# Top-k attention with a GELU block: turn copies, projections and the first pair's load put in another order

## The chip, the cores and the metric

The kernel runs on one core of a Trainium2 chip. The time is the device time of one execution in microseconds (us); the median of several executions is given. A core has five engines that each work through their own queue in order: TensorE (PE, with its weight loads shown apart as PEld), VectorE (DVE), ScalarE (ACT), GpSimd (POOL) and SyncE (SP), which here only issues transfers (DMAs). The engines wait for each other by semaphores.

## The reference

Eight batches (B) of eight heads (H), 576 rows (S) of 64 numbers (D), all 32-bit floats. For each row of q the scores against all 576 rows of k are found, only the 32 largest are kept, a softmax is taken over them, and the result is multiplied with v. The heads are laid side by side (512 numbers for each of 4608 rows), and two products with a gate between them follow.

```python
scores = scale * np.matmul(q, k.transpose(0, 1, 3, 2))
kth = np.partition(scores, -top_k, axis=-1)[..., -top_k:-top_k + 1]
scores = np.where(scores >= kth, scores, -1000000000.0)
attn = np.exp(scores - np.max(scores, axis=-1, keepdims=True))
attn = attn / (np.sum(attn, axis=-1, keepdims=True) + 1e-09)
x = np.matmul(attn, v)                    # then (B,H,S,D) -> (B*S, H*D)
h = x @ w_in                              # 512 -> 2048
out = (h * (1.0 / (1.0 + np.exp(-1.702 * h)))) @ w_out   # 2048 -> 512
```

## The kernel before, in words

**Tiles and slots.** Two heads form a pair, and a batch has four pairs. The 576 rows of a head are four blocks of 128 and a tail of 64. The attention is cut into 144 slots, 18 for a batch: a slot is one block of rows of one pair (two heads), or the tails of two pairs. Batch 0 takes block 0 of pairs 0, 1, 2, 3, then block 1 of the four pairs, and so on. The order of every instruction is written out by hand (`manual_schedule`): `opening`, then `slot(n)` for slots 0 to 11 one at a time (the single slots), then `two_slots(n)` for two at a time, then `last_slot`. Each engine executes its instructions in the order in which these functions issue them.

**The steps of a slot.** `prepare` turns q and k (rows on partitions) by TensorE so that the 64 numbers of a head lie on partitions, and ScalarE copies them out of PSUM (L202, L204; the tails L208 to L211). `scores` multiplies (TensorE, L234), `copy_scores` brings the scores to SBUF (ScalarE, L245), `topk` finds the 32 largest of each row by VectorE: four rounds of MAX8 (L254) with three of MATCH_REPLACE8 (L257) between them, 14 operations for the two heads, listed 0 to 13. In the next slot follow `bounds` (GpSimd, L273 and L274, `cut` and `low`), `exponentials` (ScalarE, Prelu L282 and Exp L284, which also gives the sums `den`), `divide` (VectorE takes the reciprocal, L293 and L295, behind operation 5 of that slot's `topk`; GpSimd scales an identity matrix by it, the tile `by`, L299). The `turn` multiplies blocks of the exponentials with `by`, which turns and divides them in one (TensorE, L315 for the two times four full blocks, L318 for the ends), and ScalarE copies the result to `pt` (L323, three copies). `values` multiplies with v (TensorE, L345), ScalarE copies the result into `xT` (L357).

**The second half.** When four pairs of a block of rows are there, `hidden` makes 512 of the 2048 hidden values (TensorE, L388, tile `ph`, one buffer), `tanh` (ScalarE, L405) and `gate` (VectorE, L421, behind operation 9 of `topk`) make `gT`, and `project` multiplies four blocks of it with `wout` (TensorE, L436, sums in `po`). In the single slots `project` is called once, from slot 8 on, if more than two gated tiles wait and the weight pieces that it reads have been finished in program order.

**The weights.** `win` and `wout` come as 32 pieces of 512 KB (`raw`, eight buffers, L125) and are worked over in slots 0 to 11, two or three pieces a slot: `size` (ScalarE, L147), `shift` (VectorE, L148), `low` and `sign` (ScalarE, L150 and L149), and in the next slot two GpSimd operations (L143, L144), which `finish_one` issues: two pieces behind operation 2 of `topk`, the others behind operation 5, after `divide`.

**A single slot's order.** ScalarE, for n of 5 to 11: Prelu and Exp of slot n-1, score copies of slot n+1, `tanh`, `size` of the pieces, `low` of the pieces, the three copies of the turn of slot n-1, `sign` of the pieces, the copy to `xT`. TensorE: `project` (from slot 8), the turn of slot n-1, `scores(n + 2)`, `values(n - 1)`, `prepare` if one is due, `hidden`. Slot 4 does the turns and values of both slots 2 and 3.

**The opening.** `stay_warm` issues TensorE products of no use. `load` issues the loads of a pair: one DMA for each of two heads to a tile `[128, 4, 2, 64]` (a partition holds four rows of each head, the two heads interleaved), one DMA for the tails. The load pool has two buffers of a name. q of pair 0 goes through SP, k of pair 0 through ScalarE's queue; then pair 1, the first two pieces of the weights, and, after `prepare_first`, `scores(0)`, `prepare` of pair 1 and `scores(1)`, the loads of pairs 2 and 3, v of pair 0 and the next two pieces. `prepare_first` turns pair 0: eight transposes, q copied by VectorE, k by ScalarE, then the tails.

Of the kernel before, what the change touches and what calls it, by code (L numbers as in the profile page):

```python
# [9 lines left out]
ALU = mybir.AluOpType  # L10
ENG = mybir.EngineType
F32 = mybir.dt.float32
# [4 lines left out]
P = 128  # L17
# [11 lines left out]
def kernel(  # L29
# [27 lines left out]
    nc = tc.nc  # L57

    B, H, S, D = q.shape
# [3 lines left out]
    NF = S // P  # L63
# [97 lines left out]
    def stay_warm(count, of=ident[:]):  # L161

        none = ps_p.tile([P, C], F32, name="none", tag="po")
        for i in range(count):
            nc.tensor.matmul(none[:, 0:P], lhsT=of, rhs=of, start=True, stop=True)

    def load(name, b, hp, queue=nc.sync):
        src = q if name == "q" else k
        t = loads.tile([P, NF, 2, D], F32, name=f"{name}_l")
        for j in range(2):  # L170
            queue.dma_start(t[:, :, j, :], src[b, 2 * hp + j, 0:FULL, :].rearrange("(p t) d -> p t d", t=NF))

        if ("ends", b, hp) not in loaded:
            loaded["ends", b, hp] = loads.tile([P, 2, D], F32, name="ends")
        on = slice(0, TAIL) if name == "q" else slice(TAIL, P)
        queue.dma_start(
            loaded["ends", b, hp][on, :, :], src[b, 2 * hp : 2 * hp + 2, FULL:S, :].rearrange("h p d -> p h d")
        )
        loaded[name, b, hp] = t
# [61 lines left out]
    def copy_scores(n):  # L241
        ps = st[n].pop("ps")
        sc = st[n]["sc"] = scp.tile([P, 2, S], F32, name="sc")
        for i in range(2):
            nc.scalar.copy(out=sc[:, i, :].rearrange("p (c k) -> p c k", c=2), in_=ps[i][:, :, 0:HALF])  # L245

    def topk(n):

        sc = st[n]["sc"]
        top = st[n]["top"] = small.tile([P, 2, TOPK], F32, name="top")  # L250
        left = lefts.tile([P, 2, S], F32, name="left")

        def largest(r, i):
            nc.vector.max(top[:, i, 8 * r : 8 * r + 8], (left if r else sc)[:, i, :])  # L254

        def remove(r, i):
            nc.vector.match_replace(  # L257
                left[:, i, :], top[:, i, 8 * r : 8 * r + 8], (left if r else sc)[:, i, :], LOWEST
            )

        ops = []
        for r in range(TOPK // 8):
            ops += [lambda r=r, i=i: largest(r, i) for i in range(2)]
            if r < TOPK // 8 - 1:
                ops += [lambda r=r, i=i: remove(r, i) for i in range(2)]
        return ops
# [58 lines left out]
    def turn_main(n):  # L325
        for i in range(2):
            turn(n, i * NF, MAIN[i], NF)

    def turn_ends(n):

        turn(n, 2 * NF, FULL, 1)
# [68 lines left out]
    def tanh(aside):  # L400

        if to_gate:
            ph, g, rows = to_gate.pop()
            th = thp.tile([P, G, P], F32, name="th")
            nc.scalar.activation(th[:], ph[:], AF.Tanh, scale=0.851 / RAISE)  # L405
            if aside:
                h = raws.tile([P, G, P], F32, name="h", tag="raw")
                nc.scalar.copy(out=h[:], in_=ph[:])
                ph = h
            gated.append((th, ph, g, rows))  # L410
# [15 lines left out]
    def project(blocks):  # L426

        if blocks[0] == 0:
            proj["on"] = to_project.pop(0)
            if proj["on"][1] == 0:  # L430
                proj["po"] = ps_p.tile([P, C], F32, name="po")
        gT, g, rows = proj["on"]
        po = proj["po"]
        for i in blocks:
            f = g * G + i
            nc.tensor.matmul(  # L436
                po[:], lhsT=gT[:, i, :], rhs=wout[:, f, :], start=(f == 0), stop=(f == FC - 1)
            )
        if blocks[-1] == G - 1 and g == NG - 1:
            ob = osp.tile([P, C], F32, name="ob")  # L440
            nc.scalar.mul(out=ob[:], in_=po[:], mul=0.5 / RAISE**2)
            for on, to in rows:
                nc.sync.dma_start(to, ob[on, :])
# [40 lines left out]
    def may_project(waiting):  # L484

        return len(to_project) > waiting and len(finished) >= NG * CC + (to_project[0][1] + 1) * G

    def prepare_first():

        both = {name: loaded.pop((name, 0, 0)) for name in ("q", "k", "ends")}  # L490
        qt = qT[0, 0] = qkt.tile([P, S], F32, name="q_t")
        kt = kT[0, 0] = qkt.tile([P, S + TAIL], F32, name="k_t")
        tp = {}
        for name in "qk":
            tp[name] = ps_t.tile([P, 512], F32, name="tp")
            for t in range(NF):
                nc.tensor.transpose(tp[name][:, t * P : (t + 1) * P], both[name][:, t, :, :], ident[:])
        nc.vector.tensor_scalar(qt[:, 0:FULL], tp["q"][:], SCALE, None, op0=ALU.mult)
        nc.scalar.copy(out=kt[:, TAIL : TAIL + FULL], in_=tp["k"][:])
        ends = ps_t.tile([P, 512], F32, name="tp")  # L500
        nc.tensor.transpose(ends[:, 0:P], both["ends"][:], ident[:])
        nc.vector.tensor_scalar(qt[:, FULL:S], ends[:, 0:TAIL], SCALE, None, op0=ALU.mult)
        for to in (0, TAIL + FULL):
            nc.vector.tensor_copy(out=kt[:, to : to + TAIL], in_=ends[:, TAIL:P])
        stay_warm(4)

    def opening():

        stay_warm(9, v_ends[0][:].rearrange("p j d -> p (j d)"))
        load("k", 0, 0, nc.scalar)  # L510
        for hp in range(2):
            for name in "qk":
                if (name, 0, hp) not in loaded:
                    load(name, 0, hp)
        for x in by_slot[0]:
            load_piece(x)
        prepare_first()
        scores(0)
        copy_scores(0)
        stay_warm(2)  # L520
        for name in "qk":
            prepare(name, 0, 1)
        early.extend(round_piece(x) for x in by_slot[0])
        for piece in early:
            piece["size"]()
        scores(1)
        copy_scores(1)
        for hp in range(2, NP):
            for name in "qk":
                load(name, 0, hp)  # L530
        load_v(0, 0)
        for x in by_slot[1]:
            load_piece(x)

    def slot(n):

        todo = later.pop(n, [])
        for fn, args in todo:
            if fn is not prepare:
                fn(*args)  # L540
        preparing = [args for fn, args in todo if fn is prepare]
        some = [round_piece(x) for x in by_slot.get(n, [])] if n else early
        if n == 0:
            for piece in some:
                piece["low"]()
                piece["sign"]()
        else:
            bounds(n - 1)
            exponentials(n - 1)
            copy_scores(n + 1)  # L550
            tanh(False)
            if 1 < n <= TURNS:
                turn_main(n - 2)
                turn_ends(n - 2)
            for piece in some:
                piece["size"]()
        for i, op in enumerate(topk(n)):
            op()
            if i == 2:
                for _ in range(min(2, len(unfinished))):  # L560
                    finish_one()
            if i == 5:
                if n > 0:
                    divide(n - 1)
                while unfinished:
                    finish_one()
            if i == 9:
                gate(False)
        for piece in some:
            piece["shift"]()  # L570
            unfinished.append(piece["finish"])
        if n > PROJECTS and may_project(2):
            project(range(G))
        if n < NP:
            for args in preparing:
                prepare(*args)
        if n > 0:
            for piece in some:
                piece["low"]()
        if n >= TURNS:  # L580
            turn_main(n - 1)
            turn_ends(n - 1)
        scores(n + 2)
        if n == SETTLED:
            copy_scores(n + 2)
        if n == 0:
            return
        for piece in some:
            piece["sign"]()
        idle = not ready and n < TURNS  # L590
        if 1 < n <= TURNS:
            values(n - 2)
        if n >= TURNS:
            values(n - 1)
        if n >= NP:
            for args in preparing:
                prepare(*args)
        if idle:
            stay_warm(8)
        hidden()  # L600
# [117 lines left out]
```

## Time and profile before

| what | value |
| --- | --- |
| median of 4 executions | 1615.65 us (1613.86 to 1617.25) |
| the profiled execution | 1617.21 us, its span in the profile 1615.4 us |
| TensorE busy | 1580.2 us, 98% |
| VectorE busy | 1474.0 us, 91% |
| ScalarE busy | 1152.7 us, 71% |
| GpSimd busy | 748.0 us, 46% |
| first product on loaded data | at 5.94 us |
| first MAX8 on VectorE | at 11.99 us |
| mean share of the 16 DMA engines, 0 to 60 us | 0.66 |

The profile comes from one execution. Its time line is in microseconds from the span's start. Busy time counts instructions that run; PEclk is the granted TensorE clock as a share of full speed. "A <- B" behind an instruction names what ended its wait. A product of 32-bit floats appears as two records, a transpose as one. A line such as `x16` merges 16 records of a kind that follow each other; the time before it is from the first start to the last end. The chain of waits follows the work back from the end, at each step to what released it.

### The profile page before, as it was taken

The numbers are of one execution on the slowest core, as the hardware profiler recorded it, in microseconds if no ns is written. First come the engines' busy times: TensorE is split into PE (matmuls) and PEld (weight loads), VectorE is DVE, ScalarE is ACT, GpSimd is POOL, SyncE is SP. The second block draws the span as 40 slices with busy tenths as digits, with TensorE's granted clock in tenths as the row PEclk, the third lists the DMA queues.
The fourth block names the chain that finished last, engine by engine and source line by source line (L and its number), as shares of the span: only waits on it lengthen the run. The fifth ranks groups of instructions, "written<-read, shape, count | busy, mean of one in ns | idle before, by whom it ended". The sixth has DMA issues, their size and how long they took to land.

```text
span 1615.4 us, 32125 instructions
## 1 busy us (share of the span) xinstructions
PE 1580.2 (98%) x12023; PEld 1182.0 (73%) x12023; DVE 1474.0 (91%) x3218; ACT 1152.7 (71%) x2441; POOL 748.0 (46%) x780
## 2 busy tenths in 40 slices
PE   7789999999999999999999999999999999999999
PEld 5676677777777777777777777777777777777776
DVE  7998999999999999999999999999999999999960
ACT  6997777777677777777777777777777777777751
POOL 3886344444444444444444444444444444444430
PEclk8899999999999999999999999999999999999999
DMA  7451100010001001110001010001000100000000
GB/s 228 134 153 36 44 22 23 20 40 15 23 15 44 23 22 30 30 43 16 23 15 44 18 27 16 23 21 44 15 22 16 44 22 23 23 8 8 8 8 14
DMA packets 100636, 56.61 MB, mean 35 GB/s; under 512 B 83584, under 2 KB 91776, under 8 KB 100480
## 3 DMA queue, kind: packets, MB, share of 16 engines
q1 hardware_dynamic: 99280, 54.25, 12.2%
q8 instruction: 95, 1.56, 0.4%
q14 instruction: 61, 0.50, 0.1%
q10 hardware_dynamic: 1200, 0.30, 0.1%
HBM read 45.09 MB, written 9.44 MB: 34 GB/s over the span
## 4 chain that ended last, share of the span: by engine, by line
PE 93%; ACT 3%; DVE 3%; issue 0%; POOL 0%; DMA 0%; SPq 0%; POOLq 0%; ACTq 0%
PE ph L388 32%; PE po L436 31%; PE o L345 10%; PE s_ps L234 10%; PE tp L313 8%; PE tp L202 2%; DVE top L254 1%; DVE left L257 1%; ACT sc L245 1%; ACT pr L284 1%; PE tp L315 1%; ACT raw L150 0%; ACT wout L147 0%; ACT sc L282 0%; DMA q_l<-in_q_dram 0%
## 5 line engine op out<-in xcount | busy, mean ns | idle before, releaser
L254 DVE MAX8 top<-left 128x8 f32<-128x576 f32 x864 | 610.2, 749 | 0.0
L436 PE MATMUL po<-wout,gT 128*128 128x512 f32 x1152 | 540.9, 594 | 3.0 <-POOL wout L144 2.3
L388 PEld LDWEIGHTS ph<-xT,win 128*128 128x128 f32 x4096 | 467.9, 192 | 40.5 <-issue 40.3
L388 PE MATMUL ph<-xT,win 128*128 128x128 f32 x4096 | 485.0, 277 | 0.0
L257 DVE MATCH_REPLACE8 left<-top,left 128x576 f32<-128x576 f32 x576 | 423.6, 744 | 0.0
L302 POOL TENSOR_SCALAR pr<-pr,rden 128x576 f32<-128x576 f32 x133 | 229.7, 1727 | 348.8 <-ACT th L405 340.3
L436 PEld LDWEIGHTS po<-wout,gT 128*128 128x128 f32 x1152 | 197.7, 191 | 148.6 <-issue 143.2
L418 POOL TENSOR_SCALAR th<-th 128x512 f32<-128x512 f32 x131 | 195.7, 1494 | 221.2 <-ACT th L405 221.2
L323 ACT COPY pt<-tp 128x512 f32<-128x512 f32 (+1 forms) x432 | 193.1, 482 | 146.3 <-PE tp L313 139.1
L282 ACT ACTIVATE sc<-sc,cut 128x576 f32<-128x576 f32 x288 | 208.3, 774 | 124.9 <-POOL cut L273 124.8
L245 ACT COPY sc<-s_ps 128x576 f32<-128x576 f32 x288 | 169.7, 643 | 72.5 <-PE s_ps L234 72.2
L284 ACT ACTIVATE pr<-sc,low 128x576 f32<-128x576 f32 x288 | 219.5, 766 | 0.0
L313 PEld LDWEIGHTS tp<-ident,pr 128*128 128x128 f32 x1197 | 143.1, 141 | 102.2 <-issue 56.1
L257 DVE MATCH_REPLACE8 left<-top,sc 128x576 f32<-128x576 f32 x288 | 212.0, 745 | 0.0
L254 DVE MAX8 top<-sc 128x8 f32<-128x576 f32 x288 | 202.4, 746 | 3.2 <-ACT sc L245 3.2
L234 PE MATMUL s_ps<-k_t,q_t 64*128 64x288 f32 (+1 forms) x1280 | 181.5, 430 | 0.3 <-ACT k_t L204 0.3
L313 PE MATMUL tp<-ident,pr 128*128 128x128 f32 x1197 | 174.2, 273 | 0.0
L419 POOL TENSOR_TENSOR gT<-th,h 128x512 f32<-128x512 f32 x131 | 167.0, 1275 | 10.9
L345 PE MATMUL o<-pt,v_l 128*64 128x128 f32 (+1 forms) x2560 | 159.2, 268 | 0.7
L345 PEld LDWEIGHTS o<-pt,v_l 128*64 128x64 f32 x2560 | 131.5, 138 | 32.5 <-ACT pt L323 13.5
L273 POOL TENSOR_SCALAR cut<-top 128x2 f32<-128x2 f32 x144 | 40.1, 278 | 229.2 <-DVE top L254 229.2
L234 PEld LDWEIGHTS s_ps<-k_t,q_t 64*128 64x128 f32 (+1 forms) x1280 | 98.7, 177 | 59.3 <-issue 41.8
(65 smaller groups left out, 1171.3 us busy)
## 6 DMA issues: line engine op xcount, KB each, us to landing
q_l<-in_q_dram SPq DMA_DIRECT2D x64, 128.0 KB, 3.2
raw<-in_moe_w_in_dram SPq DMA_DIRECT2D x16, 512.0 KB, 5.1
v_l<-in_v_dram SPq DMA_DIRECT2D x32, 256.0 KB, 3.0
raw<-in_moe_w_out_dram SPq DMA_DIRECT2D x16, 512.0 KB, 3.4
out_dram<-ob SPq DMA_DIRECT2D x32, 256.0 KB, 2.3
k_l<-in_k_dram SPq DMA_DIRECT2D x62, 128.0 KB, 3.1
ends<-in_q_dram SPq DMA_DIRECT2D x32, 32.0 KB, 2.6
v_e<-in_v_dram SPq DMA_DIRECT2D x64, 16.0 KB, 2.6
```

The costliest lines, as they stand in the source:

```text
L234: nc.tensor.matmul(ps[i][rows, c, 0:HALF], lhsT=qT[b, hps[p]][on, cols], rhs=kT[b, hps[p]][on, FIRST[i] + c * HALF : FIRST[i] + (c + 1) * ...
L254: nc.vector.max(top[:, i, 8 * r : 8 * r + 8], (left if r else sc)[:, i, :])
L257: nc.vector.match_replace(left[:, i, :], top[:, i, 8 * r : 8 * r + 8], (left if r else sc)[:, i, :], LOWEST)
L282: nc.scalar.activation(sc[:, i, :], sc[:, i, :], AF.Prelu, bias=cut[:, i : i + 1], alpha=HUGE)
L284: nc.scalar.activation(pr[:, i * S : (i + 1) * S], sc[:, i, :], AF.Exp, bias=low[:, i : i + 1], accum_out=den[:, i : i + 1],)
L302: nc.gpsimd.tensor_scalar(pr[:, S : 2 * S], pr[:, S : 2 * S], rden[:, 1:2], None, op0=ALU.mult)
L313: nc.tensor.transpose(tp[:, c * P : (c + 1) * P], pr[:, at], ident[:])
L323: nc.scalar.copy(out=to, in_=tp[:, 0 : blocks * P])
L345: nc.tensor.matmul(o[j * D : (j + 1) * D, 0 : cols.stop - cols.start], lhsT=main[:, j, c, :] if c < NF else tail[:, j, :], rhs=pt[:, j * N ...
L388: nc.tensor.matmul(ph[:, i, :], lhsT=win[:, c, f * P : (f + 1) * P], rhs=xT[:, c, :], start=(c == 0), stop=(c == CC - 1),)
L418: nc.gpsimd.tensor_scalar(th[:], th[:], 1.0, None, op0=ALU.add)
L436: nc.tensor.matmul(po[:], lhsT=gT[:, i, :], rhs=wout[:, f, :], start=(f == 0), stop=(f == FC - 1))
```

## The change

The opening:

- `load` gets a second layout, used when a queue is named: the tile is `[128, 2, 4, 64]`, with the two heads apart, so that the four rows of a head lie together in a partition. Pair 0 of q (on SP) and of k (on ScalarE's queue) is loaded so; all other loads keep the old layout.
- Pair 0 is turned by products with the identity, one for each head and block (`both_heads`), in place of a transpose of both heads. `prepare_first` turns only the first block of q and all of k; the tails go through `ph`. The new `prepare_rest`, called after `scores(1)` and `copy_scores(1)`, turns the other three blocks of q, and one ScalarE operation copies them. The first buffers of pair 0 are given up there.
- `stay_warm(9)` becomes `stay_warm(8)`.

The single slots:

- ScalarE: `tanh` goes behind the sizes of the pieces. From slot 4 on the copies of the turn of slot n-1 go ahead of `low`.
- VectorE: `gate` goes behind operation 10 of `topk` in place of 9.
- TensorE: `project` goes from ahead of the turn to behind `values` and `prepare`, ahead of `hidden`.

`two_slots` and `last_slot` are unchanged.

```diff
-    def load(name, b, hp, queue=nc.sync):
+    def load(name, b, hp, queue=None):
...
-        t = loads.tile([P, NF, 2, D], F32, name=f"{name}_l")
+        t = loads.tile([P, NF, 2, D] if queue is None else [P, 2, NF, D], F32, name=f"{name}_l")
+        heads_of = (lambda j: t[:, :, j, :]) if queue is None else (lambda j: t[:, j, :, :])
+        queue = queue or nc.sync
         for j in range(2):
-            queue.dma_start(t[:, :, j, :], src[b, 2 * hp + j, 0:FULL, :].rearrange("(p t) d -> p t d", t=NF))
+            queue.dma_start(heads_of(j), src[b, 2 * hp + j, 0:FULL, :].rearrange("(p t) d -> p t d", t=NF))
...
+    def both_heads(to, src, t):
+        for j in range(2):
+            nc.tensor.matmul(to[j * D : (j + 1) * D, t * P : (t + 1) * P], lhsT=src[:, j, t, :], rhs=ident[:])
...
     def prepare_first():
-        for name in "qk":
-            tp[name] = ps_t.tile([P, 512], F32, name="tp")
-            for t in range(NF):
-                nc.tensor.transpose(tp[name][:, t * P : (t + 1) * P], both[name][:, t, :, :], ident[:])
-        nc.vector.tensor_scalar(qt[:, 0:FULL], tp["q"][:], SCALE, None, op0=ALU.mult)
...
+        some, full = [ps_t.tile([P, 512], F32, name="tp") for _ in range(2)]
+        ends = ps_h.tile([P, G, P], F32, name="ph")
+        both_heads(some, loaded["q", 0, 0], 0)
+        for t in range(NF):
+            both_heads(full, loaded["k", 0, 0], t)
+        nc.tensor.transpose(ends[:, 0, :], loaded["ends", 0, 0][:], ident[:])
+        nc.vector.tensor_scalar(qt[:, 0:P], some[:, 0:P], SCALE, None, op0=ALU.mult)
+        nc.scalar.copy(out=kt[:, TAIL : TAIL + FULL], in_=full[:])
...
+    def prepare_rest():
+        full = ps_t.tile([P, 512], F32, name="tp")
+        for t in range(1, NF):
+            both_heads(full, loaded["q", 0, 0], t)
+        nc.scalar.mul(out=qT[0, 0][:, P:FULL], in_=full[:, P:FULL], mul=SCALE)
+        for name in ("q", "k", "ends"):
+            del loaded[name, 0, 0]
...
     def opening():
-        stay_warm(9, v_ends[0][:].rearrange("p j d -> p (j d)"))
+        stay_warm(8, v_ends[0][:].rearrange("p j d -> p (j d)"))
+        load("q", 0, 0, nc.sync)
         load("k", 0, 0, nc.scalar)
...
         scores(1)
         copy_scores(1)
+        prepare_rest()
...
             copy_scores(n + 1)
-            tanh(False)
             if 1 < n <= TURNS:
                 turn_main(n - 2)
                 turn_ends(n - 2)
             for piece in some:
                 piece["size"]()
+            tanh(False)
...
-            if i == 9:
+            if i == 10:
                 gate(False)
...
-        if n > PROJECTS and may_project(2):
-            project(range(G))
         if n < NP:
             for args in preparing:
                 prepare(*args)
+        if n >= TURNS:
+            turn_main(n - 1)
+            turn_ends(n - 1)
         if n > 0:
             for piece in some:
                 piece["low"]()
-        if n >= TURNS:
-            turn_main(n - 1)
-            turn_ends(n - 1)
         scores(n + 2)
...
         if n >= NP:
             for args in preparing:
                 prepare(*args)
+        if n > PROJECTS and may_project(2):
+            project(range(G))
         if idle:
             stay_warm(8)
         hidden()
```

More of the change, by code (lines that the diff above doesn't have):

```diff
@@ L486, in may_project @@
         return len(to_project) > waiting and len(finished) >= NG * CC + (to_project[0][1] + 1) * G
+    def both_heads(to, src, t):
+        for j in range(2):
+            nc.tensor.matmul(to[j * D : (j + 1) * D, t * P : (t + 1) * P], lhsT=src[:, j, t, :], rhs=ident[:])
     def prepare_first():
-        both = {name: loaded.pop((name, 0, 0)) for name in ("q", "k", "ends")}
         qt = qT[0, 0] = qkt.tile([P, S], F32, name="q_t")
         kt = kT[0, 0] = qkt.tile([P, S + TAIL], F32, name="k_t")
-        tp = {}
@@ L494, in prepare_first @@
-        for name in "qk":
-            tp[name] = ps_t.tile([P, 512], F32, name="tp")
-            for t in range(NF):
-                nc.tensor.transpose(tp[name][:, t * P : (t + 1) * P], both[name][:, t, :, :], ident[:])
-        nc.vector.tensor_scalar(qt[:, 0:FULL], tp["q"][:], SCALE, None, op0=ALU.mult)
-        nc.scalar.copy(out=kt[:, TAIL : TAIL + FULL], in_=tp["k"][:])
-        ends = ps_t.tile([P, 512], F32, name="tp")
-        nc.tensor.transpose(ends[:, 0:P], both["ends"][:], ident[:])
@@ L502, in prepare_first @@
-        nc.vector.tensor_scalar(qt[:, FULL:S], ends[:, 0:TAIL], SCALE, None, op0=ALU.mult)
+        some, full = [ps_t.tile([P, 512], F32, name="tp") for _ in range(2)]
[5 more added lines that the diff above has]
+        nc.vector.tensor_scalar(qt[:, 0:P], some[:, 0:P], SCALE, None, op0=ALU.mult)
@@ L503, in prepare_first @@
+        nc.scalar.copy(out=kt[:, TAIL : TAIL + FULL], in_=full[:])
         for to in (0, TAIL + FULL):
-            nc.vector.tensor_copy(out=kt[:, to : to + TAIL], in_=ends[:, TAIL:P])
+            nc.vector.tensor_copy(out=kt[:, to : to + TAIL], in_=ends[:, 0, TAIL:P])
+        nc.vector.tensor_scalar(qt[:, FULL:S], ends[:, 0, 0:TAIL], SCALE, None, op0=ALU.mult)
         stay_warm(4)
+    def prepare_rest():
[5 more added lines that the diff above has]
+            del loaded[name, 0, 0]
```

## The prediction

> **What bounds the kernel now.** I read the page's busy line and slices first, then busy time slot by slot, then the chain and the timelines of 54 to 160 us.
>
> ```profile
> PE 1580.2 (98%) x12023; PEld 1182.0 (73%) x12023; DVE 1474.0 (91%) x3218; ACT 1152.7 (71%) x2441; POOL 748.0 (46%) x780
> PE   7789999999999999999999999999999999999999
> ```
>
> TensorE is the bound, and from 160 us on it has no hole: it works 1349.31 of the 1350 us from 200 to 1550. Its 35.2 us of idleness lie nearly all in the first 160 us (17.2 before 60 us, 11.4 from 60 to 140, 2.4 from 140 to 200). So the change is worth the microseconds by which TensorE reaches the end of slot 11 earlier. The table has a row for each of slots 4 to 11, cut where ScalarE begins a slot's Prelu (length, then busy PE, PEld, DVE, ACT, POOL, clock, DMA):
>
> ```profile
> 54.90:68.70 13.80, 11.30 (x103) 9.66 (x102) 13.77 (x32) 12.20 (x26) 12.76 (x14) 0.88 0.43 145
> 68.70:81.30 12.60, 9.76 (x80) 8.35 (x80) 10.76 (x26) 11.00 (x24) 9.17 (x10) 0.89 0.39 125
> 81.30:92.90 11.60, 9.09 (x82) 7.88 (x82) 10.56 (x23) 11.13 (x24) 8.80 (x10) 0.97 0.42 138
> 92.90:104.40 11.50, 8.68 (x83) 7.47 (x82) 11.46 (x27) 11.04 (x24) 9.94 (x11) 1.00 0.54 162
> 104.40:116.20 11.80, 11.80 (x91) 8.94 (x90) 11.77 (x27) 11.20 (x24) 10.27 (x11) 1.00 0.62 174
> 116.20:128.00 11.80, 11.80 (x91) 8.94 (x90) 11.76 (x29) 11.22 (x24) 10.15 (x11) 1.00 0.62 176
> 128.00:144.00 16.00, 13.66 (x90) 9.90 (x90) 15.06 (x30) 9.39 (x20) 11.28 (x13) 0.89 0.01 1
> 144.00:155.80 11.80, 10.12 (x96) 8.91 (x95) 8.85 (x21) 10.81 (x24) 5.68 (x8) 1.00 0.00 1
> ```
>
> Slots 5 and 6 have idle VectorE and TensorE: ScalarE is late. Slots 8 and 9 are full TensorE. Slot 10 lasts 16 us. The chain and the PE timeline give the causes:
>
> ```profile
> 74.86 1.67 ACT raw L150 x3
> 76.53 0.47 ACT pt L323
> 77.00 0.04 issue
> 77.05 0.44 PE tp L318 x4
> ```
>
> In slots 5, 6, 7 and 11 the three `low` copies (L150) stand ahead of the turn's copies.
>
> ```profile
> 136.37 1.97 PE L436 MATMUL po<-wout,gT 128*128 128x512 f32 x2 [2.34 <-POOL wout L144]
> ```
>
> In slot 10 the projection stands first on TensorE and waits 2.34 us for the last weight piece, which GpSimd finishes after `by`.
>
> **Part 1, slots 4 to 11.** Rows of a slot: ScalarE Prelu and Exp 2.9 us to the sums, score copies 1.05, sizes 1.72, tanh 0.5, turn copies 0.49+0.49+0.27, low 1.68, sign 1.75, xT 0.17. TensorE turn 1.78+0.4, scores 1.17, values 1.24, projection 3.44, hidden 3.77. VectorE 11.5 with nothing waited for (91.90 to 103.41). GpSimd does two pieces (2.65 each) ahead of `by`, so `by` begins 5.56 after VectorE's slot start D (97.45 after 91.90; 108.97 after 103.41), and the turn can begin at D+6.1.
>
> Slot 4: the turn is late itself (L315 from 60.91, 3.35 us at half clock), so ScalarE, which spent that wait on `low`, now waits: Prelu of slot 5 at about 69.0, 0.25 later. Slot 5: tanh goes behind the sizes (0.5 for 1.72, no sum); the pt copies start at 75.1 instead of 76.42, the end turns, scores and values follow, and `low` and `sign` run beside them. Values end at 79.7 (81.06) and sign at 79.75, so Prelu of slot 6 starts at 80.0, not 81.24. VectorE stalled 1.81 and 1.00 us for the sums in slots 5 and 6; the first stays, the second goes. D is then 79.3 in slot 6 (79.04), 90.85 in slot 7 (91.90), 102.35 in slot 8 (103.41): a gain of 1.06, after which VectorE is the bound. The gate's move by one replacement (0.73) is hidden: it must free `ph` before `hidden`, some 1.5 us later in slots 5 to 7, behind the projection after that.
>
> Slot 8: TensorE has nothing ahead of the turn now. It used to do the projection from 107.75 to 111.18, which covered the wait for `by`; now it idles from 105.4 to 102.35+6.1 = 108.45. Then 2.18+1.17+1.24+3.44+3.77 = 11.8 a slot: turns at 108.45, 120.2, 132.0 and 143.8. VectorE's D+6.1 is 119.95, 131.5 and 142.9, so `by` is in time. In slot 10 the weight piece is finished at 135.0, and the projection now comes at 136.6: the 2.34 us wait is gone, and the 1.9 us of half clock behind it. In slot 11, 0.63 (`by`) and 1.05 (`low` ahead of pt) go. Its hidden ends at 143.8+8.9 = 152.7, against 158.23: **-5.5 us**. The queues behind are no nearer: VectorE and GpSimd gain 5 to 6 us too, and the last pieces, at about 154.2, come before the block that needs them (155.7).
>
> The clock is the price. The gaps before the turn join up: 2.2 us in slot 6, 3.1 in slot 7, 3.0 in slot 8.
>
> ```profile
> 134.00:136.30 2.30, 0.03 (x1) 0.00 (x0) 2.30 (x5) 0.66 (x2) 2.22 (x2) 1.00 0.00 0
> 136.30:141.00 4.70, 4.63 (x20) 3.48 (x22) 4.70 (x11) 0.61 (x2) 2.06 (x4) 0.64 0.00 0
> ```
>
> A gap of 2.3 us was followed by a clock of 0.64; one of 2.15 us (74.9 to 77.05) by 0.51; those of 2.1 and 1.7 us (87.7, 96.4) by 1.00. The spell at 136.37 cost 1.11 (two projection records 1.97 for 0.86) and 0.82 (turn 2.60 for 1.78), 1.9 us. In slot 8 it counts whole, in slot 7 only by 0.3, for there VectorE bounds. I take the middle: **+1.1 us**.
>
> The Trainium skill, "TensorE: Matmul & The Clock Gate", Part 1, says that the clock falls to half after an idle window of about 3.4 us that runs freely; the trace's gaps of 2.15 and 2.3 us sufficed. By the page gaps of 3 us are a border case; with the spell the sum of slots would be -3.6, without it -5.5.
>
> **Part 2, the opening.** Now TensorE waits until 5.94 for q (256-byte pieces, 223 GB/s from 3.0 to 5.5 us at full DMA share), and VectorE starts at 11.99. Afterwards a partition's line of a head is 1 KB. The nearest rows are `v_l` (1 KB lines, twice the bytes, 3.0 us to landing against 3.2) and the weights (382 GB/s from 22 to 28 us), so the pair lands by about 4.6, and the eight warming products end at 1.03+16x0.234 = 4.8 (18 took 4.21): start 1.1 earlier. In place of eight transposes (1.94) come ten pairs of half-width products, 20 records. At half clock 20 such records took 2.35 (values at 78.70), at full clock 1.24. Thus scores begin 0.8 earlier if TensorE stays cold (1.71 for the warming products behind as before), and 2.0 if it is warm by then. I take 1.4 and keep both ends. VectorE's smaller q and ScalarE's copy lie beside this.
>
> The skill's same page, Part 4, says that transposes do not count as work for the clock; the trace has cold transposes (0.24 us) until 8.3 and warm work from 9.92, and cannot tell. By it the 2.0 would be likelier.
>
> The added `prepare_rest` is six products (0.72) and one copy (about 0.45) in ScalarE's idle 2.91 before slot 1. But it keeps q's first buffer (two buffers of `q_l`), and the load of pair 2 must now wait for it:
>
> ```profile
> 8.24 1.22 SPq L171 DMA_DIRECT2D q_l<-in_q_dram  x2
> 18.48 2.76 SPq L125 DMA_DIRECT2D raw<-in_moe_w_in_dram  x5
> ```
>
> This load moves from 8.24 to the end of the rest, about 15.0 (scores(1) end 14.98, less 0.8, plus 0.72). Everything behind it on SP follows at the same 10.2 us: the weights of slot 1 issue at 25.2 and 25.7 instead of 18.48. Landing took 4.7 and 5.3 us there, so 29.9 and 31.0. ScalarE is in order: sizes (end 31.6), pair 3 copies 1.5, low and sign 2.3, Prelu at 35.4, sums at 38.3. VectorE's division in slot 2 stood at 36.99, so at 36.2: a stall of 2.1 us (ScalarE had 1.70+1.0 of slack). Rows for landing run from 3.8 to 7.9, so the stall from 0.6 to 4.7. Pair 2's copies end near 22.0 and don't delay VectorE. Later weights land some 6 us before use. Opening: 2.1-1.4 = **+0.7 us**.
>
> **Sum.** -5.5+1.1+0.7 = -3.7 us. The profiled execution took 1617.21 (span 1615.4) and would take 1613.5; against the median of 1615.65 that is **1612.0**. 0.2% is 3.2 us, about what a measurement of this kernel can tell from no change.
>
> **Rivals.** First, clock and queue are kind: no spell that counts, start 2.0 earlier, stall 0.6: -5.5-2.0+0.6 = -6.9, 1608.7. For it: two gaps of about 2 us left the clock at 1.00. Against: these are 3 us. Second, the late weights eat it: start only 0.8 earlier, landing 7.9, stall 4.7: -5.5+1.1+3.9 = -0.5, 1615.1. For it: five weight loads together took up to 9.3 us. Against: the first two of them took 4.7 and 5.3. Third, slower: the joined gaps put TensorE at half clock in each of slots 5 to 8, where turn, scores and values then are late and so the next slot's sums. Price 1.9 each, and from the third on it outweighs the 5.5: -5.5+7.6+1.3 (cold start) = +3.4, 1619.0. For it: 2.15 us sufficed once. Against: slots 6 and 7 have VectorE as cover. That the edits do not reach the program is excluded: in the changed order of instructions the projection does stand behind the values and the copies ahead of `low`.
>
> **Chances.** Forecast 0.55, kind 0.15, eaten 0.18, slower 0.12. The forecast's own spread (1.5 us either way) leaves 0.35 of its 0.55 beyond 0.2%: faster 0.35+0.15 = 0.50, same 0.20+0.18 = 0.38, slower 0.12. Range 1608.7 (kind) to 1617.0 (past eaten, most of slower left out).
>
> **What would show it.** Right: slot 10 lasts under 12.5 us, no wait for `wout` L144; slots 5 and 6 about 11.3 each; a TensorE gap near 3 us before slot 8's turn; VectorE's first MAX8 near 10.6; SP's third pair of q issues near 15 and VectorE waiting in slot 2 for sums. Wrong: that stall is absent, first MAX8 later than 11.5, or the clock below 0.6 in several of slots 5 to 9.

## The result and the profile after

| | before | after |
| --- | --- | --- |
| median | 1616.41 us (58 executions) | 1613.33 us (40 executions) |
| ratio | | 0.9980, 95% interval 0.9976 to 0.9985 |
| profiled execution, its span | 1617.21, 1615.4 us | 1613.58, 1611.8 us |
| first MAX8 | 11.99 us | 9.01 us |
| end of `hidden` in slot 11 with the turn of k behind it | 158.61 us | 155.13 us |

3.2 us by the ratio, where 3.7 were forecast. The forecast's sum held; two of its three terms (slots, clock, opening) did not. Below, a ratio step of 0.001 is 1.6 us; runs made at different times are compared by their ratios to the kernel before, which ran beside them.

The page of the kernel after, its busy line and its clock in 40 slices:

```profile
PE 1579.2 (98%) x12045; PEld 1181.4 (73%) x12045; DVE 1472.1 (91%) x3218; ACT 1152.9 (72%) x2442; POOL 747.9 (46%) x780
PEclk8889999999999999999999999999999999999999
```

TensorE is still the bound, with the same 1349.31 busy us from 200 to 1550. Nearly all of the difference, 3.5 of the 3.6 us between the two spans, is there at the end of slot 11. The chain of the kernel before begins with the opening, and the one of the kernel after below it (start, length, what):

```profile
1.47 4.33 DMA q_l<-in_q_dram
...
5.94 1.94 PE tp L497 x8
...
8.28 1.71 PE none L165 x8
9.99 1.35 PE s_ps L234 x8
...
11.99 1.41 DVE top L254 x2
```

```profile
1.03 3.71 PE none L165 x16
4.74 1.24 PE tp L494 x20
5.99 0.26 PE ph L505
6.25 0.89 PE none L165 x8
7.14 1.22 PE s_ps L237 x8
8.36 0.63 ACT sc L248
...
9.01 1.41 DVE top L257 x2
```

There is no DMA on it any more: the pair has landed when the warming products (those of `stay_warm`) end. The 20 records that turn pair 0 (the first block of q and all of k) took 1.24 us, what the prediction gave for full clock, and the eight warming products behind them 0.89 in place of 1.71. VectorE begins 2.98 us earlier. Of the span's 3.6 us that leaves 0.6 for slots 4 to 11, where 5.5 less a spell of 1.1 had been counted. The table by slot of the kernel after (length, busy PE, PEld, DVE, ACT, POOL, clock, DMA; slots 4, 5, 6, 8, 9, 10) shows why:

```profile
51.90:66.30 14.40, 10.87 (x92) 9.07 (x91) 14.37 (x33) 12.03 (x26) 12.61 (x13) 0.76 0.43 139
66.30:77.20 10.90, 9.64 (x91) 8.43 (x91) 8.38 (x20) 10.85 (x23) 7.69 (x10) 1.00 0.44 144
77.20:90.90 13.70, 10.43 (x85) 9.22 (x84) 13.67 (x32) 11.10 (x25) 12.05 (x12) 0.88 0.34 117
...
101.90:115.70 13.80, 10.53 (x71) 8.53 (x70) 13.77 (x33) 11.07 (x23) 11.96 (x12) 0.75 0.54 159
115.70:128.50 12.80, 12.80 (x92) 9.42 (x91) 10.52 (x25) 11.19 (x24) 9.03 (x11) 1.00 0.52 152
128.50:139.20 10.70, 10.70 (x87) 8.40 (x86) 10.15 (x23) 9.51 (x21) 7.90 (x9) 1.00 0.01 2
```

Slot 10 has shrunk from 16.0 to 10.7 us, as forecast, and slot 5 from 12.6 to 10.9. But slots 4, 6 and 8 are long, and each has a low clock. (A stretch in which TensorE runs at half clock is called a spell below; TensorE is warm at full clock and cold at half.) TensorE's timeline has the turns of slots 6 and 8 with the gaps in front of them, first in the kernel before, then in the kernel after:

```profile
85.67 2.05 PE L315 MATMUL tp<-by,pr 128*128 128x128 f32 x16 [0.44 <-POOL by L299]
...
111.18 1.95 PE L315 MATMUL tp<-by,pr 128*128 128x128 f32 x16
```

```profile
82.94 3.68 PE L318 MATMUL tp<-by,pr 128*128 128x128 f32 x16 [3.27 <-POOL by L302]
...
107.55 3.78 PE L318 MATMUL tp<-by,pr 128*128 128x128 f32 x16 [3.27 <-POOL by L302]
```

The turn takes 1.95 to 2.05 us at full clock, and in the kernel after 3.7 to 3.8 behind 3.27 us without work. It is `by` (GpSimd) that it waits for. Slot 4 had a spell before as well (13.8 us, clock 0.88; now 14.4 and 0.76): there 0.77 us without work stand in front of the turn, and 2.76 a little earlier.

### The profile page after: what moved, and what is told of

Its sections match the earlier page's. It is cut to its first block, busy times and chain, and to the rows that moved or that the text cites. A ratio compares the mean times of both kernels' runs of the same rounds, so it can differ in the third digit from the quotient of the medians.

```text
span 1611.8 us, 32168 instructions
## 1 busy us (share of the span) xinstructions
PE 1579.2 (98%) x12045; PEld 1181.4 (73%) x12045; DVE 1472.1 (91%) x3218; ACT 1152.9 (72%) x2442; POOL 747.9 (46%) x780
## 4 chain that ended last, share of the span: by engine, by line
PE 93%; DVE 4%; ACT 2%; issue 0%; POOL 0%; POOLq 0%; ACTq 0%
PE ph L391 32%; PE po L439 31%; PE s_ps L237 10%; PE o L348 9%; PE tp L316 8%; DVE top L257 2%; DVE left L260 2%; PE tp L205 2%; PE tp L318 1%; ACT sc L248 1%; PE none L165 0%; DVE win L148 0%; PE tp L211 0%; ACT raw L150 0%; ACT raw L149 0%
## 5 line engine op out<-in xcount | busy, mean ns | idle before, releaser
L422 POOL TENSOR_TENSOR gT<-th,h 128x512 f32<-128x512 f32 x131 | 167.0, 1275 | 10.9
```

## The experiments

Theory A is what the two traces say: the opening brings most, and half-clock spells behind joined gaps eat most of what the slots gain. Theory B is the prediction's sum.

**1. The opening alone.** The function `slot` of the kernel before in the kernel after.

> The opening's edits alone, the single slots as before. Theory A (as the two traces read: VectorE begins 3.0 us earlier and nothing is lost in slots 1 to 3): 2.9 us less than before, first MAX8 near 9.0. Theory B (the prediction's sum: earlier start 1.4, late weights 2.1): 0.7 us more than before, VectorE waiting in slot 2.

Measured: ratio 0.9989 (0.9980 to 0.9998), 1.8 us less; first MAX8 at 9.87, and VectorE waits for nothing in slot 2. B's loss in the opening is not there. A's 2.9 still lies in the interval, but it came from a favourable pair of traces: the first MAX8 moves with the clock from execution to execution. In the three profiled executions that have the opening of before it came at 11.99, 10.31 and 10.70, in the nine with the new one between 8.81 and 10.23. Means 11.0 and 9.5: a start 1.5 us earlier.

**2. The slots alone.** The function `slot` of the kernel after in the kernel before.

> The single slots' edits alone, the opening as before. Theory A (spells of half clock in slots 4, 6 and 8 eat the gain): 0.6 us less than before, and the clock near 0.5 behind TensorE gaps of about 3 us. Theory B (prediction): 4.4 us less than before with one spell of 1.1.

Measured: ratio 0.9987 (0.9978 to 0.9996), 2.1 us less: between both theories. Slot 6 had its spell (13.42 us, clock 0.87), and slot 7 had one too (11.27 us, 0.85), behind a gap of 1.96 us. Slot 8 had none (11.70 us, 1.00) although the gap in front of it was 2.26 us. So the same order of work meets a different clock in different executions.

**3. The projection ahead of the turn again.** In `slot` of the kernel after, the two lines go back:

```diff
+        if n > PROJECTS and may_project(2):
+            project(range(G))
         if n < NP:
...
-        if n > PROJECTS and may_project(2):
-            project(range(G))
         if idle:
```

> The changed kernel with the projection back ahead of the turn, all else changed. Theory A (the gap that the projection leaves in slot 8 costs 3.0 in clock there, but the wait for the last weight piece in slot 10 and its own spell return, 2.3 and 1.9): about 1 us more than the changed kernel, slot 8 at full clock. Theory B (the move itself is the gain, the clock costs little): 4 us more than the changed kernel.

Measured: ratio 0.9996 (0.9987 to 1.0005), 2.6 us more than the kernel after, between the theories. Slot 8 keeps its clock (11.98 us, 1.00), slot 6 does not (13.38), and in slot 10 the wait for the weight piece is back with 2.67 us, and a clock of 0.89 behind it.

**4. The gaps filled.** The kernel after, with one addition at the end of `slot`:

```diff
         hidden()
+        if TURNS < n <= PROJECTS:
+            stay_warm(8)
```

> The changed kernel with eight products of no use behind the hidden product of slots 5, 6 and 7 (1.9 us at full clock), which fill most of TensorE's gaps of 3.27, 1.94 and 3.27 us and delay nothing that waits for GpSimd. Theory A (a gap of 3 us halves the clock for 4 to 5 us): no spell in slots 6 and 8, 3.0 us less than the changed kernel. Rival (the spells follow a clock's own rhythm or the load, not the gap): the spells stay and the time is within 0.5 us of the changed kernel.

Measured: 1609.61 us, ratio 0.9967 (0.9954 to 0.9979), 2.1 us less than the kernel after by the ratios, with intervals that overlap a little; the two profiled executions are 5.3 us apart, and that of run 4 is the fastest of its five. Its table by slot, the same six slots:

```profile
51.70:65.50 13.80, 11.52 (x104) 9.77 (x103) 13.77 (x32) 12.20 (x26) 12.75 (x14) 0.87 0.41 144
65.50:76.40 10.90, 9.74 (x92) 8.53 (x91) 9.04 (x21) 10.85 (x23) 7.55 (x9) 1.00 0.44 144
76.40:88.40 12.00, 10.52 (x99) 9.38 (x98) 11.97 (x28) 11.02 (x24) 10.46 (x11) 1.00 0.41 134
...
99.90:111.40 11.50, 10.37 (x89) 8.52 (x88) 11.47 (x27) 11.00 (x23) 9.96 (x11) 1.00 0.56 169
111.40:123.20 11.80, 11.80 (x90) 8.94 (x89) 11.77 (x27) 11.18 (x24) 10.25 (x11) 1.00 0.62 185
123.20:133.80 10.60, 10.60 (x87) 8.38 (x86) 10.46 (x25) 9.43 (x20) 8.89 (x11) 1.00 0.01 2
```

TensorE does more work, of no use, and is faster: slots 6 to 8 stay at a clock of 1.00 and last 12.0, 11.5 and 11.5. The gaps that are left in front of their turns are 1.48, 1.12 and 1.13 us, and the turns take 2.05. The rival falls: with the gaps the spells are gone, and runs 8 and 9 below, which have the same filling and more, lie clear of the kernel after. In this execution the slots give what the prediction's walk gave without a spell: the span is 8.9 us shorter than before's, of which VectorE's earlier start is 3.2, so the slots bring 5.7 (walk: 5.5). By the ratios it is less: 5.3 us, less a mean start of 1.5, leave 3.8, with an interval of about 2 us either way. Against the kernel after the eight slots are 5.2 us shorter (95.4 for 100.6); that is what the clock cost in that one execution.

**5. Old layout, transposes.** Pair 0 loaded interleaved and turned by transposes, the rest of q still later:

```diff
-        t = loads.tile([P, NF, 2, D] if queue is None else [P, 2, NF, D], F32, name=f"{name}_l")
-        heads_of = (lambda j: t[:, :, j, :]) if queue is None else (lambda j: t[:, j, :, :])
+        t = loads.tile([P, NF, 2, D], F32, name=f"{name}_l")
+        heads_of = lambda j: t[:, :, j, :]
...
-        for j in range(2):
-            nc.tensor.matmul(to[j * D : (j + 1) * D, t * P : (t + 1) * P], lhsT=src[:, j, t, :], rhs=ident[:])
+        nc.tensor.transpose(to[:, t * P : (t + 1) * P], src[:, t, :, :], ident[:])
```

> The changed kernel with pair 0 loaded in the old interleaved layout and turned by transposes again (the other blocks of q still later). Landing theory (1 KB lines land 1.1 us earlier than 256-byte pieces): TensorE's first work on data at 5.8 to 5.9, and the first MAX8 at 10.0 to 11.7 by the clock's state; 1.0 to 1.5 us more than the changed kernel. Rival (products wake the clock and transposes do not): as above, but always cold up to the warming products, so first MAX8 near 11.7 and later than in the run with products by 1.0 or more.

**6. Old layout, products.** The first half of that edit, and `lhsT=src[:, t, j, :]`.

> The changed kernel with pair 0 in the old interleaved layout, turned by products as in the change. Landing theory: TensorE's first work on data at 5.8 to 5.9 in place of 4.74, about 1.1 us more than the changed kernel. Rival (the warming products end at 4.8 anyway and the layout is worth nothing): first work at 4.8, same time within 0.3 us.

Measured: both 0.9983 (0.9973 and 0.9974 to 0.9992), no difference from the kernel after that can be told, so neither the expected 1.0 to 1.5 us nor the rivals are settled by the time. The later landing is there: 2.7 to 2.9 us from issue for q of pair 0 in the new layout, 3.4 to 4.7 in run 6, where the first head's product starts at 4.75 and the second head's waits until 6.23. The first MAX8 came at 11.53 (transposes, cold until 10.7) and 10.56 (products, warm). But in run 6 the 1.55 us of later start were made up in slots 4 to 9, where the spells were shorter. That transposes keep the clock down is not shown: in run 2 they ran at 0.16 us each, full speed, behind warming products that were cold like those of run 5. What wakes the clock at the start is left open.

**7. Pair 2's load held back.** One product of no use behind the rest reads pair 1's q, so that its buffer is given up late too:

```diff
+        pair_1 = loaded["q", 0, 1]
         for name in "qk":
             prepare(name, 0, 1)
...
         prepare_rest()
+        stay_warm(1, pair_1[:, 0, :, :].rearrange("p j d -> p (j d)"))
```

> The changed kernel with one product of no use that reads pair 1's q behind the rest of pair 0, so that both buffers are taken and pair 2's load has to wait for the rest, as the prediction had it. Prediction's mechanism: pair 2's load issues near 13.0 in place of 9.42, the weights of slot 1 near 23.3 in place of 19.76; of these 3.5 us ScalarE has 1.05 to spare, so VectorE waits 2.4 us for the sums in slot 2, and the kernel takes about 2.4 us more than the changed one. Rival (the loads have slack that the prediction missed): same time within 0.5 us.

Measured: ratio 1.0002 (0.9993 to 1.0011), 3.6 us more than the kernel after; the traces differ by 2.0. SP's queue in the kernel after and then in this run, then the wait of VectorE in this run from 30 to 40 us, and last what that load waited for in the kernel after:

```profile
9.42 1.23 SPq L174 DMA_DIRECT2D q_l<-in_q_dram  x2
...
19.76 2.65 SPq L125 DMA_DIRECT2D raw<-in_moe_w_in_dram  x5
```

```profile
12.90 1.23 SPq L174 DMA_DIRECT2D q_l<-in_q_dram  x2
...
23.40 2.65 SPq L125 DMA_DIRECT2D raw<-in_moe_w_in_dram  x5
```

```profile
DVE some L296 <- ACT pr L287: 2.0, 1, 2.0
```

```profile
SPq L174 <- PE tp L205: 2.2, 1, 2.2
```

So the mechanism of the prediction is real and its size about right (2.4 expected; 2.0 of waiting and between the traces, 3.6 by the ratios). In the kernel after it does not happen: the load goes at 9.42, when the transposes of pair 1's q (L205, 8.79 to about 9.4) have run, and before the rest of pair 0 begins at 11.99. It took the buffer that came free first, which is pair 1's. In the program, too, pair 1 is turned ahead of the rest of pair 0; no run parts the program's order from the order in time.

**8. Gaps of slots 3 and 4 filled too.** In run 4's kernel, `if n > 2: stay_warm(10)` between `turn_main(n - 2)` and `turn_ends(n - 2)`.

> The kernel with filled gaps, with ten more products of no use between the main turn and the ends in slots 3 and 4, where TensorE waits 3.4 and 2.8 us for ScalarE's copy. If the half-clock turn of slot 4 (3.78 us in place of 1.95) comes from that gap: slot 4 ends 1.8 us earlier, VectorE's wait in slot 5 shrinks by that, 1.5 to 1.8 us less than the kernel with filled gaps. Rival (slot 4 is held by GpSimd's scaling of the identity, not by the clock): same time within 0.5 us.

Measured: 1608.38 us, ratio 0.9956 (0.9943 to 0.9968), 1.8 us less than run 4 but with intervals that overlap; the profiled span is that of run 4 (1606.6 for 1606.5). Slot 4 is no shorter (13.74 us, clock 0.88): gaps of 1.35 and 1.02 us stay behind the filling, and the turn took 2.75 us.

**9. All of them filled.** Fifteen products there, and `if n > 3: stay_warm(4)` behind `turn_ends(n - 2)`.

> The kernel with more filled gaps, with fifteen in place of ten products between main turn and ends in slots 3 and 4, and four behind the ends of slot 4, so that no gap over 0.6 us stands ahead of the turn of slot 4. If the clock holds that turn (2.75 us and 1.85 for the scores in place of 1.95 and 1.24): 1.4 us less than the kernel with more filled gaps. Rival (held by GpSimd): no change within 0.5 us.

Measured: 1608.70 us, ratio 0.9950 (0.9935 to 0.9965), not told from run 8. The clock did hold slot 4: the turn takes 2.05, the slot 12.51 us. But slots 5 and 6 last 11.27 and 12.31 in place of 10.95 and 11.98, so from the start of slot 4 on the run gains 0.6. VectorE is the bound there (busy 12.28 of 12.31 us in slot 6).

**10. The projection moved alone.** The kernel before with the move of run 3 the other way, nothing else.

> The kernel before with one edit, the projection behind the values in the single slots. If the clock is the price of the move: a TensorE gap near 3 us before the turn of slot 8 and a spell behind it in some executions, no wait for the last weight piece in slot 10; net between 0 and 3 us less than before. The prediction's walk without spells would give: slot 10's 4.2 and slot 11's 0.6 less, slot 8's lost cover 3.4 more, so 1.4 us less.

Measured: ratio 1.0020 (1.0011 to 1.0030), 3.2 us more than before. The expectation was wrong, and not by the clock, which is 1.00 from slot 7 on; the gap in front of slot 8's turn is 1.71 us and not near 3. ScalarE's longest waits from 100 to 150 us of this run, and below it the same line of the kernel after (110 to 150):

```profile
ACT th L405 <- PE ph L388: 9.0, 3, 3.0
```

```profile
ACT th L408 <- PE ph L391: 3.3, 3, 1.7
```

Where the projection stands between the values and `hidden`, the hidden values come 3.5 us later behind the values (114.3 to 117.8 us), and `tanh` waits for them. With `tanh` at its old place the sizes, the low words and the turn's copies queue behind it, so TensorE waits 2.71, 1.60 and 1.60 us for `pt` in slots 9 to 11. The changed kernel takes that away with two edits: `tanh` behind the sizes, and the copies ahead of the low words. Run 12, which has only the first of the two, still waits 1.06, 0.51 and 0.51 us in these places.

**11 and 12. Both orders at full clock.** Run 4's kernel with the projection ahead (filled in slots 5 and 6 alone), and with the low words ahead of the copies.

> The changed kernel with the projection back ahead of the turn and eight products of no use in slots 5 and 6, so that both orders of the projection can be compared at full clock (the other is the kernel with filled gaps). Walk of the prediction: the wait of 2.34 us in slot 10 and the 0.63 us in slot 11 are back, cover in slot 8 too; at full clock the place of the projection alone is worth 1 to 3 us, so 1 to 3 us more than the kernel with filled gaps. Rival (the place is worth nothing once the clock is kept): within 0.7 us of it.

> The kernel with filled gaps, with the low words ahead of the turn's copies again from slot 4 on. Walk of the prediction: VectorE waits again in slots 5 and 6, 1.1 us more up to slot 8, and 1.05 us more in slot 11: 1 to 2 us more than the kernel with filled gaps. Rival (the copies' place is worth nothing, since slot 4 loses what slots 5 and 6 gain): within 0.7 us.

Measured: ratios 0.9975 (0.9964 to 0.9986) and 0.9979 (0.9970 to 0.9989), so 1.3 and 1.9 us more than run 4, both in the expected bounds, with intervals that overlap run 4's: the times alone do not exclude the rivals. The traces speak against them: slots 5 to 11, all at a clock of 1.00, last 83.9 and 85.1 us, in run 4 81.7 (slot 4 is at 0.77 in both and 0.87 in run 4, and is left out). The waits are the expected ones: 2.56 us for the weight piece in the first; in the second 7.9 us for `pt` in seven places, with slots 9, 10 and 11 at 12.90, 12.34 and 13.84 (run 4: 11.77, 10.64, 13.31).

## Why the prediction was right, and where it was not

- **Slots without the clock, -5.5:** the walk fits run 4's trace, which is at full clock in slots 5 to 11 and gives 5.7. Slot 10's wait is gone, slot 5 is 10.9 us, and VectorE is the bound in slots 6 to 8. As a mean the size is less sure: 3.8 by the ratios, about 2 either way.
- **The clock, +1.1:** the mis-sized term. The prediction expected gaps of 2.2, 3.1 and 3.0 us in slots 6 to 8 and took one spell at the middle of 0.3 and 1.9. The trace has spells in slots 4, 6 and 8, behind gaps of 3.27 us in the last two, and against run 4 they cost 5.2 between the two traces, 2.1 by the ratios. Two points failed. The spell at slot 8's turn lasted 5 us and cost 2.9, not 1.9: the turn, the ends and the scores are all at half speed. And a late slot makes the next gap: late values make late sums, VectorE then waits, and GpSimd's `by` with it. VectorE's waits for the sums in slots 5, 7 and 9 are 2.5, 1.5 and 1.7 us; in run 4 they are 1.8, 0 and 0, and slots 6 to 8 are even. In run 2 slot 8 had no spell, so the times of a kernel can contain both cases.
- **The start, -1.4:** right as a mean (1.5 from three and nine traces, which spread over 1.7 and 1.4). The two traces shown differ by 3.0, because the one of before was cold and the one of after warm. The upper end of 2.0 was too low for such a pair: it left the eight warming products behind the turn at their cold 1.71 us, and they took 0.89.
- **The late weights, +2.1:** wrong. The step that failed is "it keeps q's first buffer (two buffers of `q_l`), and the load of pair 2 must now wait for it". The load waits for whichever buffer of the two comes free first, and that is pair 1's, at 9.4. Run 7 shows that the price of the step was about right had it been so. That VectorE does not wait in slot 2 was one of the prediction's own signs of being wrong.
- **`tanh`, no cost:** about right for the changed kernel, but for a reason that was not seen. The prediction did not count that `hidden` comes later for `tanh`. Run 10 shows that the projection's move loses 3.2 us without the other edits; with them it gains 2.6 (run 3).
- The total of -3.7 is close to -3.2 because two errors cancel. Alone, the opening measured -1.8 where +0.7 was forecast (run 1), and the slots with their clock -2.1 where -4.4 was forecast (run 2). The late weights counted too much (2.1) and the clock too little by about as much. That is luck, and the right sum does not support the terms.
- The rival in which the joined gaps halve the clock in slots 5 to 8 had the right mechanism; it counted four spells of 1.9, and the trace has two of these, which cost 1.6 (slot 6) and 2.9 (slot 8) on TensorE.

The Trainium skill's "TensorE: Matmul & The Clock Gate", Part 1, has the clock fall after an idle window of about 3.4 us that runs freely. In slots 5 to 11 of the runs here all ten gaps of 3.2 us or more were followed by half clock. Of the shorter ones, 1.96 us (run 2), 2.18 and 2.34 (both in the kernel before; the prediction reads the first as 2.15) and 2.67 (run 3) were; 1.94 (the kernel after), 2.26 (run 2), 2.56 (run 11) and 2.71 (run 10) were not. None of these gaps is as long as the page's window, so its length does not hold here. That the same length of gap meets both cases fits a window that runs freely and speaks against a fixed length of the gap; what the window counts no run shows.

## What to carry to other kernels

A gap on a bound engine has a second price where its clock falls behind it: gaps joined to one of 3 us can cost nearly as much as the waiting that the change removed (5.2 of 5.7 us between the traces), and work of no use in the gap can win it back (run 9, the change with the gaps filled, is 8 us faster than the kernel before, ratio 0.9950). When work is moved ahead of a producer, look for who waits for that producer and what is queued behind the waiter; edits that look separate may only pay together. And where a ring has several buffers, ask which one comes free first before a load is said to wait.

## What the hardware showed that was not expected

The clock column reads 1.00 for the first 8 us of both profiles, though the warming products took 0.23 us a record there and 0.11 to 0.12 us once warm; the durations tell the state, the column does not. The same opening was warm at 4.5 to 5 us in some executions and only while k was being turned in others (20 records in 1.24 to 2.33 us). Over the nine traces with this opening VectorE's start moves by up to 1.4 us.
